# Chunk 0 of a fused attention and gated-MLP kernel: deviations sent through DRAM, k taken row by row, loads and transposes reordered

## The chip, the cores and the metric

The kernel runs on one core of a Trainium2 chip. The metric is the device time of one execution in microseconds. The core's engines are TensorE (PE; its weight loads are shown as PEld), VectorE (DVE), ScalarE (ACT), GpSimd (POOL) and SyncE (SP). Each works through its own instructions in their order and waits on counters (semaphores) that others raise. DMA transfers are issued from the queue of SP, ACT or POOL and raise a counter when they have landed.

## The reference, cut to what matters

```python
# x: 2048 tokens x 1024, 32 heads of 32, window of 8 keys, 2 apart; F = 3584; all bf16
xn  = (x - mean(x)) / sqrt(var(x) + 1e-5)            # layer norm over the 1024
q, k, v = split_heads(xn @ wqkv)                     # wqkv: 1024 x 3072
logits[s, w] = q[s] . k[s - 2 w] / sqrt(32)          # w = 0..7, masked where s - 2 w < 0
s   = (softmax(logits) @ v[s - 2 w]) @ wo
g   = silu((silu(B_x @ w1) * (B_x @ w3)) @ w2)      # here B_x is xn
out = x + s * g
```

## The kernel before

Tokens go in four chunks of 512 (`CH`), a chunk in four tiles of 128 tokens. For each chunk TensorE computes q, k and v, the gate and up products, the down product and the output projection, one behind the other; the windowed attention runs beside it on VectorE, ScalarE and GpSimd from a list of side work with costs and due times (`Side`). The schedule is written out by hand: every engine's order is the order of the source, except that counters, of which the DMA transfers of SP and ACT share eight in turn, are given out when the program is built. A transfer that gets a counter waits until that counter's last transfer has landed.

Chunks 1 to 3 get their normalised, transposed input while the chunk before them runs. Chunk 0 has nothing before it, and its opening (L161 to L204 and L511 to L670) is code of its own. The change lies there alone.

*Loads.* SP issues the transfers in the order of L161 to L166: tiles 0 and 1 of x in two halves each, then the weights of q (wq, four tiles of two rows, a "row" being 128 of the 1024 input features) and of k (wk, likewise), one transfer of 256 KB for a row (`cuts=2`), with tiles 2 and 3 of x in between. Both wq and wk carry the name wq in the profile.

*Tokens 0 to 255 (tiles 0 and 1).* To start before the deviations are known, TensorE transposes the raw tiles, takes off the mean, and the result `xcT` is centred but not divided by the deviation. q and k of these 256 tokens are made from `xcT` by `part` (L602), which for a row `kt` and output groups `js` issues one matmul of 256 columns a group into that group's PSUM bank: eight banks (`banks`), q in the left half of a bank and k in the right. The reciprocal deviations `rs0` (a column of 128 partitions for each tile) must then multiply the columns; `proj_out` (L294) does so on VectorE while it empties the bank, with `R`, a 128 x 256 tile that holds the 256 values in every partition. `R` is made on the chip itself: GpSimd splits each value into three bf16 parts (L618 to L621), VectorE spreads them on diagonals (`dgr`, L627), TensorE sums them over the partitions with three matmuls against ones into a free half of the last bank (L632), and ScalarE copies the bank to `R` (L636).

q runs over all eight rows for all groups (L622 to L626); k over rows 0 to 4 for all groups, and then, group by group, rows 5 to 7, after which the group's bank is emptied (L655 to L661).

*Tokens 256 to 511 (tiles 2 and 3).* These are normalised on VectorE (`stats`, `std` on ScalarE, `recip`, `norm0`) and transposed by DMA into `xnT` (L646), all four tiles from SP in the order 2, 3, 0, 1; behind these stand the loads of v's weights (`wv`, L651) and the next weights. q and k of tokens 256 to 511 then go group by group, 256 columns wide (L662 to L668), into the bank halves that `proj_out` has emptied, and ScalarE empties them again. v follows for all 512 tokens (L673, matmuls at L264), and needs all four tiles of `xnT` and `wv`.

Of the kernel before, what the change touches and what calls it, by code (L numbers as in the profile page):

```python
# [8 lines left out]
FP32 = mybir.dt.float32  # L9
BF16 = mybir.dt.bfloat16  # L10
# [35 lines left out]
def kernel(  # L46
# [11 lines left out]
    nc = tc.nc  # L58
    P = 128
    S, D, F = 2048, 1024, 3584  # L60
    Dh, W, DIL = 32, 8, 2
    KT = D // P
    CH = 512
# [5 lines left out]
    NJ = 8  # L69
# [19 lines left out]
    small = ctx.enter_context(tc.tile_pool(name="small", bufs=4))  # L89
# [5 lines left out]
    blk = ctx.enter_context(tc.tile_pool(name="blk", bufs=9))  # L95
    sm = ctx.enter_context(tc.tile_pool(name="sm", bufs=1))
    ep = ctx.enter_context(tc.tile_pool(name="ep", bufs=2))
    ctx.enter_context(tc.manual_schedule())

    side = Side()  # L100
# [16 lines left out]
    def load_w(n=1, cuts=1, between=None):  # L117
        for _ in range(n):
            item = next(w_next, None)
            if item is None:  # L120
                return
            wt = wstream.tile([P, 2048], BF16, tag="w", name="w" + item[0])
            if item[0] == "q":
                _, t, a = item
                view = wt.rearrange("p (k c) -> p k c", k=2)
                src = wqkv_r[:, 2 * a:2 * a + 2, t * D:(t + 1) * D]
            elif item[0] == "2":
                _, dh, fb = item
                view = wt.rearrange("p (i n) -> p i n", n=512)
                src = w2_r[:, fb * 4:(fb + 1) * 4, dh * 512:(dh + 1) * 512]  # L130
            else:
                view = wt.rearrange("p (k f) -> p k f", k=KT)
                src = (w1_r if item[0] == "1" else w3_r)[:, :, item[1] * 256:(item[1] + 1) * 256]
            step = view.shape[1] // cuts
            for i in range(cuts):
                if i > 0 and between is not None:
                    between()
                nc.sync.dma_start(out=view[:, i * step:(i + 1) * step, :], in_=src[:, i * step:(i + 1) * step, :])  # L138
            w_tiles.append((item, view))
# [14 lines left out]
    x0 = [xp.tile([P, D], BF16, tag="x", name=f"x0_{st}") for st in range(NST)]  # L154

    def load_x0(st, cuts=1):
        w = D // cuts
        for h in range(cuts):
            nc.sync.dma_start(out=x0[st][:, h * w:(h + 1) * w], in_=x_flat[st * P:(st + 1) * P, h * w:(h + 1) * w])  # L159

    load_x0(0, 2)  # L161
    load_x0(1, 2)
    load_w(3, cuts=2)
    load_w(1, cuts=2, between=lambda: load_x0(2))
    load_x0(3)
    load_w(4, cuts=2)  # L166
    eps_t = const.tile([P, 1], FP32, name="eps_t")
    nc.vector.memset(eps_t[:], 1e-5)
    warm = hp.tile([P, CH], BF16, tag="ht", name="warm")
# [3 lines left out]
    ident = const.tile([P, P], BF16, name="ident")  # L173
    nc.gpsimd.memset(ident[:], 0.0)
    nc.gpsimd.affine_select(
        out=ident[:], in_=ident[:], compare_op=ALU.not_equal, fill=1.0,
        base=0, pattern=[[-1, P]], channel_multiplier=1,
    )
    ones_b = hp.tile([P, P], BF16, tag="ht", name="ones_b")
# [4 lines left out]
        out=ident_d[:], in_=ident_d[:], compare_op=ALU.not_equal, fill=-1.0 / D,  # L184
# [5 lines left out]
        out=maskb[:], in_=maskb[:], compare_op=ALU.is_ge, fill=-1.0e9,  # L190
# [17 lines left out]
    def half_stats(x_t, stats, i):  # L208
        nc.vector.bn_stats(out=stats[:, i, :], in_=x_t[:, i * 512:(i + 1) * 512])

    def normalize(x_t, mean, rstd):
        nc.vector.tensor_scalar(
            out=x_t[:], in0=x_t[:], scalar1=mean, scalar2=rstd, op0=ALU.subtract, op1=ALU.mult,
        )
# [74 lines left out]
    def proj_out(t, j, ps, a=0, b=CH, by=None):  # L289
        dst = (qT[:, j, a:b], kT[:, j, HALO + a:HALO + b], vT[:, j, HALO + a:HALO + b])[t]  # L290
        if by is None:
            nc.scalar.copy(out=dst, in_=ps)  # L292
        else:
            nc.vector.tensor_mul(dst, ps, by)  # L294
# [219 lines left out]
    HC = CH // 2  # L514
    xcT = xnT_pool.tile([P, KT, CH], BF16, tag="xnT", name="xcT")
# [6 lines left out]
    V, A = nc.vector.tensor_copy, nc.scalar.copy  # L522
    mv0 = [small.tile([P, 2], FP32, tag="mv0", name=f"mv0_{st}") for st in range(NST)]
    st0 = {st: small.tile([P, 2, nc.vector.BN_STATS_DIM], FP32, tag="st0", name=f"st0_{st}") for st in range(1, NST)}
    rs0 = small.tile([P, NST], FP32, tag="rs0", bufs=1, name="rs0")
    dgs = [hp.tile([P, P], BF16, tag="ht", name=f"dg{st}") for st in range(2)]
    tot = small.tile([P, 1], FP32, tag="tot", bufs=1)
    nm = small.tile([P, 1], FP32, tag="nm", bufs=1)
    rsb = small.tile([P, 3, 2], BF16, tag="rsb", bufs=1, name="rsb")
    rest = small.tile([P, 2], FP32, tag="rest", bufs=1, name="rest")  # L530
    junk = ep.tile([P, D], BF16, tag="gt", bufs=5, name="junk")
    dgr = ep.tile([P, 3, 2, P], BF16, tag="gt", bufs=5, name="dgr")
    R = ep.tile([P, HC], FP32, tag="gt", bufs=5, name="R")

    def stats(st):
        half_stats(x0[st], st0[st], 0)
        half_stats(x0[st], st0[st], 1)
        nc.vector.bn_aggr(out=mv0[st][:], in_=st0[st][:])

    def std(st):  # L540
        nc.scalar.activation(out=rs0[:, st:st + 1], in_=mv0[st][:, 1:2], func=ACTF.Sqrt, bias=eps_t[:], scale=1.0)

    def recip(a, b):
        nc.vector.reciprocal(out=rs0[:, a:b], in_=rs0[:, a:b])

    def norm0(st):
        normalize(x0[st], mv0[st][:, 0:1], rs0[:, st:st + 1])
# [22 lines left out]
    def copy_in(src, st, k0, n, eng):  # L570
# [13 lines left out]
        out=dgs[1][:], in0=ident[:], scalar1=mv0[1][:, 0:1], scalar2=-1.0, op0=ALU.mult, op1=ALU.mult,  # L584
# [14 lines left out]
    banks = [psum_mm.tile([P, CH], FP32, tag="mm", name="ps_qkv") for _ in range(6)]  # L599
    banks[4:4] = [psum_aux.tile([P, CH], FP32, tag="aux", name="ps_qkv") for _ in range(2)]  # L600

    def part(t, kt, js, a, b, first, src):  # L602

        for j in js:
            o = t * HC + a % HC
            nc.tensor.matmul(  # L606
                banks[j][:, o:o + b - a], lhsT=(wq, wk)[t](kt, j), rhs=src[:, kt, a:b],
                start=first, stop=(kt == KT - 1), skip_group_check=True,
            )
# [5 lines left out]
    recip(0, 2)  # L615
    norm0(0)
    norm0(1)
    for i in range(3):  # L618
        nc.gpsimd.tensor_copy(out=rsb[:, i, :], in_=rs0[:, 0:2] if i == 0 else rest[:])
        if i < 2:  # L620
            nc.gpsimd.tensor_sub(rest[:], rs0[:, 0:2] if i == 0 else rest[:], rsb[:, i, :])  # L621
    part(0, 0, range(6), 0, P, True, xcT)  # L622
    part(0, 0, range(6), P, HC, False, xcT)
    part(0, 0, range(6, NJ), 0, HC, True, xcT)
    for kt in range(1, KT):
        part(0, kt, OPEN, 0, HC, False, xcT)  # L626
    nc.vector.tensor_mul(  # L627
        dgr[:].rearrange("p i a b -> p (i a) b"), ident[:].unsqueeze(1).to_broadcast([P, 6, P]),
        rsb[:].rearrange("p i a -> p (i a)").unsqueeze(2).to_broadcast([P, 6, P]),
    )  # L630
    for i in range(3):
        nc.tensor.matmul(  # L632
            banks[NJ - 1][:, HC:CH], lhsT=ones_b[:], rhs=dgr[:, i, :, :].rearrange("p a b -> p (a b)"),
            start=(i == 0), stop=(i == 2), skip_group_check=True,
        )
    A(out=R[:], in_=banks[NJ - 1][:, HC:CH])  # L636
    stats(2)
    std(2)
    stats(3)
    std(3)  # L640
    for st in (2, 3):
        recip(st, st + 1)
        norm0(st)
    xnT = xnT_pool.tile([P, KT, CH], BF16, tag="xnT", name="xnT_0")
    for st in (2, 3, 0, 1):
        nc.sync.dma_start_transpose(out=xnT[:, :, st * P:(st + 1) * P], in_=x0[st][:])  # L646
    wv = []
    for a in range(4):
        if a % 2 == 0:
# [2 lines left out]
        wv.append(two[:, a % 2])  # L652
    wv = by_group(wv)
    load_w(1)
    for kt in range(5):  # L655
        part(1, kt, OPEN, 0, HC, kt == 0, xcT)
    for j in OPEN:
        for kt in range(5, KT):
            part(1, kt, (j,), 0, HC, False, xcT)
        proj_out(0, j, banks[j][:, 0:HC], 0, HC, R[:])  # L660
        proj_out(1, j, banks[j][:, HC:CH], 0, HC, R[:])  # L661
    for t in range(2):  # L662
        for j in OPEN:
            for kt in range(KT):
                part(t, kt, (j,), HC, CH, kt == 0, xnT)
            if j == NJ - 1:
                load_w(4)
            proj_out(t, j, banks[j][:, t * HC:(t + 1) * HC], HC, CH)  # L668
# [3 lines left out]
    for c in range(NCH):  # L672
# [20 lines left out]
        if c + 1 < NCH:  # L693
# [10 lines left out]
            xnT = att["x"]  # L704
# [35 lines left out]
```

## Time and profile before

| What | us |
|---|---|
| median of 3 runs | 814.91 (814.81 to 815.32) |
| the profiled execution | 814.77 |
| its span, first to last instruction | 813.0 |
| start of q and k from `xnT` | 21.55 |
| start of v | 35.52 |
| granted clock of TensorE, share | 0.999 |

The span starts with the first instruction; some 1.8 us of the execution lie around it. Times in the views below are counted from the span's start. "SPq" and "ACTq" are the queues in which SP and ACT issue transfers. In a chain of waits each line is what ended last at that point, in order of time; in the timeline neighbouring instructions of a kind are merged into one line with their number (x3).

### The profile page before, as it was taken

The numbers are of one execution on the slowest core, as the hardware profiler recorded it, in microseconds if no ns is written. First come the engines' busy times: TensorE is split into PE (matmuls) and PEld (weight loads), VectorE is DVE, ScalarE is ACT, GpSimd is POOL, SyncE is SP. The second block draws the span as 40 slices with busy tenths as digits, with TensorE's granted clock in tenths as the row PEclk, the third lists the DMA queues.
The fourth block names the chain that finished last, engine by engine and source line by source line (L and its number), as shares of the span: only waits on it lengthen the run. The fifth ranks groups of instructions, "written<-read, shape, count | busy, mean of one in ns | idle before, by whom it ended". The sixth has DMA issues, their size and how long they took to land.

```text
span 813.0 us, 9680 instructions
## 1 busy us (share of the span) xinstructions
PE 807.7 (99%) x3883; PEld 411.4 (51%) x3883; DVE 473.0 (58%) x488; ACT 187.8 (23%) x310; POOL 93.9 (12%) x180
## 2 busy tenths in 40 slices
PE   9999999999999999999999999999999999999998
PEld 7954444444665444444466444444446644444443
DVE  4489573962239766495124967569411695649632
ACT  3331241012332133101133213310223321311120
POOL 1000404001100122200010022210001003040010
PEclk9999999999999999999999999999999999999999
DMA  9945989842366699984244779996434377687500
GB/s 285 292 122 163 223 203 260 284 145 74 118 189 171 197 208 187 278 266 144 79 151 133 205 195 205 191 319 208 140 91 155 104 207 193 170 227 240 181 31 21
DMA packets 195357, 147.44 MB, mean 181 GB/s; under 512 B 23536, under 2 KB 176240, under 8 KB 195312
## 3 DMA queue, kind: packets, MB, share of 16 engines
q1 hardware_dynamic: 189872, 134.76, 60.3%
q0 software_dynamic: 5440, 12.07, 6.3%
q8 instruction: 30, 0.49, 0.3%
q14 instruction: 15, 0.12, 0.1%
HBM read 130.02 MB, written 4.19 MB: 165 GB/s over the span
## 4 chain that ended last, share of the span: by engine, by line
PE 97%; DMA 1%; SPq 1%; DVE 0%; issue 0%; DVEq 0%
PE gu L264 48%; PE acc L476 21%; PE ps_qkv L264 17%; PE ps_wo L431 7%; PE acc L499 3%; PE ps_qkv L606 2%; DMA wq<-in_A_wqkv_dram 1%; DMA x<-in_A_x_dram 1%; SPq L138 0%; SPq L159 0%; DVE o_t L457 0%; DVE gt L456 0%; DVEq L456 0%
## 5 line engine op out<-in xcount | busy, mean ns | idle before, releaser
L264 PE MATMUL gu<-xnT_next,w 128*128 128x512 bf16 x1344 | 290.6, 379 | 0.0
L264 PEld LDWEIGHTS <-w 128*128 128x128 bf16 x1792 | 175.2, 98 | 211.4
L476 PE MATMUL acc<-w,ht 128*128 128x512 bf16 x784 | 170.4, 379 | 0.0
L270 DVE TENSOR_TENSOR ht<-sg,gu 128x512 bf16<-128x512 bf16 x112 | 75.8, 682 | 110.3 <-PE gu L264 93.7
L268 ACT ACTIVATE sg<-gu 128x512 bf16<-128x512 f32 x112 | 66.1, 597 | 268.9 <-PE gu L264 266.0
L264 PE MATMUL ps_qkv<-xnT_next,wq 128*128 128x512 bf16 x576 | 124.8, 379 | 0.0
L476 PEld LDWEIGHTS <-ht 128*128 128x128 bf16 x784 | 76.7, 98 | 92.5
L321 DVE TENSOR_TENSOR prod<-qT,kT 128x4096 bf16<-128x4096 bf16 x32 | 73.1, 2285 | 80.1 <-ACT kT L292 80.1
L264 PEld LDWEIGHTS <-wq 128*128 128x128 bf16 x576 | 82.6, 143 | 41.8
L264 PE MATMUL gu<-xnT,w 128*128 128x512 bf16 x448 | 96.9, 379 | 0.0
L456 DVE TENSOR_TENSOR gt<-gt,s_sb 128x512 f32<-128x512 f32 x31 | 21.4, 690 | 106.9 <-ACT gt L450 69.2
L352 POOL DMA_DIRECT2D L<-E x64 | 37.2, 587 | 282.8 <-DVE E L336 197.3
L405 DVE TENSOR_TENSOR pv<-Pr,vT 128x4096 bf16<-128x4096 bf16 x28 | 63.0, 2283 | 0.0
L332 DVE TENSOR_TENSOR prod<-prod 128x2048 bf16<-128x2048 bf16 x64 | 61.1, 955 | 1.4
L431 PE MATMUL ps_wo<-wo,oT 128*128 128x512 bf16 (+1 forms) x264 | 56.1, 373 | 0.0
L450 ACT ACTIVATE gt<-acc 128x512 f32<-128x512 f32 x32 | 19.1, 597 | 150.2 <-PE acc L476 128.4
L394 POOL DMA_DIRECT2D Pr<-pb x64 | 36.6, 579 | 107.3 <-DVE pb L386 97.2
L458 POOL DMA_DIRECT2D out_dram<-o_t x28 | 15.3, 546 | 289.3 <-DVE o_t L457 289.3
L431 PEld LDWEIGHTS <-oT 128*128 128x128 bf16 x264 | 25.8, 98 | 29.7
L416 DVE TENSOR_TENSOR oT<-oT,pv 128x4096 bf16<-128x4096 bf16 x16 | 36.6, 2289 | 0.4
L443 ACT CAST s_sb<-ps_wo 128x512 bf16<-128x512 f32 x31 | 18.1, 585 | 66.4 <-PE ps_wo L431 66.4
L606 PEld LDWEIGHTS <-wq 128*128 128x128 bf16 x262 | 28.2, 144 | 0.6 <-DMA wq<-in_A_wqkv_dram 0.5
(82 smaller groups left out, 344.0 us busy)
## 6 DMA issues: line engine op xcount, KB each, us to landing
w<-in_B_w_dram SPq DMA_DIRECT2D x168, 512.0 KB, 5.2
wq<-in_A_wqkv_dram SPq DMA_DIRECT2D x36, 512.0 KB, 3.7
wo<-in_A_wo_dram SPq DMA_DIRECT2D x8, 1024.0 KB, 11.0
wq<-in_A_wqkv_dram SPq DMA_DIRECT2D x16, 256.0 KB, 5.3
L<-E POOLq DMA_DIRECT2D x64, 64.0 KB, 6.7
Pr<-pb POOLq DMA_DIRECT2D x64, 64.0 KB, 6.4
xres<-in_A_x_dram SPq DMA_DIRECT2D x4, 1024.0 KB, 6.8
out_dram<-o_t POOLq DMA_DIRECT2D x28, 128.0 KB, 2.0
```

The costliest lines, as they stand in the source:

```text
L264: nc.tensor.matmul(ps, lhsT=lhs(kt), rhs=rhs(kt), start=(kt == 0), stop=(kt == KT - 1))
L268: nc.scalar.activation(out=sg[:], in_=g_ps[:], func=ACTF.Silu)
L270: nc.vector.tensor_mul(ht[:], sg[:], u_ps[:])
L321: nc.vector.tensor_mul(prod, qT[:], kT[:, :, o:o + CH])
L332: nc.vector.tensor_add(prod[:, 0:n, :], prod[:, 0:n, :], prod[:, n:2 * n, :])
L352: nc.gpsimd.dma_start(out=L4[sq * NH:(sq + 1) * NH, r, :, :], in_=E_r[r, :, :, sq * P:(sq + 1) * P],)
L394: nc.gpsimd.dma_start(out=Pr_r[r, :, :, sq * P:(sq + 1) * P], in_=pb[sq * NH:(sq + 1) * NH, :, :],)
L405: nc.vector.tensor_mul(dst, Pr[:, w, :].unsqueeze(1).to_broadcast([P, NJ, CH]), vT[:, :, o:o + CH])
L416: nc.vector.tensor_add(a, a, b)
L431: nc.tensor.matmul(ps[:, 0:w], lhsT=oT[:, j, st * P:(st + 1) * P], rhs=was[dh][:, j, n0:n0 + w], start=(j == 0), stop=(j == NJ - 1),)
L476: nc.tensor.matmul(accs[st][:], lhsT=hts[f][:, st * P:(st + 1) * P], rhs=w2t[:, i, :], start=(f == 0), stop=(f == FT - 1),)
L606: nc.tensor.matmul(banks[j][:, o:o + b - a], lhsT=(wq, wk)[t](kt, j), rhs=src[:, kt, a:b], start=first, stop=(kt == KT - 1), skip_group_ch ...
```

## The change

- The loads of wq are not broken any more by tiles 2 and 3 of x: all four wq tiles come first, tile 2 stands between the two rows of the first wk tile, tile 3 after it, and then the other wk rows.
- `R` is made by DMA: ScalarE's queue stores the 2 x 128 reciprocal deviations to a tile in DRAM (`rrow`, element by element transposed), and loads it back with every partition reading the same 256 values. The GpSimd split, `dgr`, the three matmuls and ScalarE's copy are gone.
- VectorE takes tile 3's statistics in two halves, with tile 2's reciprocal and normalisation between them.
- The transpose of tile 3 is issued from ScalarE's queue; tiles 2, 0 and 1 stay on SP.
- k of tokens 0 to 255 goes over rows 0 to 6 for all groups, then row 7 group by group.
- q of tokens 256 to 511 in groups 0 and 1 is made in two steps of 128 columns, tile 2 first for both groups, then tile 3.

```diff
+    dram = ctx.enter_context(tc.tile_pool(name="dram", bufs=1, space=bass.MemoryType.DRAM))
...
-    load_w(3, cuts=2)
+    load_w(4, cuts=2)
     load_w(1, cuts=2, between=lambda: load_x0(2))
     load_x0(3)
-    load_w(4, cuts=2)
+    load_w(3, cuts=2)
...
-    for i in range(3):
-        nc.gpsimd.tensor_copy(out=rsb[:, i, :], in_=rs0[:, 0:2] if i == 0 else rest[:])
-        if i < 2:
-            nc.gpsimd.tensor_sub(rest[:], rs0[:, 0:2] if i == 0 else rest[:], rsb[:, i, :])
+
+    rrow = dram.tile([2, P], FP32, name="rrow")
+    nc.scalar.dma_start(out=rrow.rearrange("s p -> p s"), in_=rs0[:, 0:2])
+    nc.scalar.dma_start(out=R[:], in_=rrow.rearrange("s p -> (s p)").unsqueeze(0).to_broadcast([P, HC]))
...
-    nc.vector.tensor_mul(
-        dgr[:].rearrange("p i a b -> p (i a) b"), ident[:].unsqueeze(1).to_broadcast([P, 6, P]),
-        rsb[:].rearrange("p i a -> p (i a)").unsqueeze(2).to_broadcast([P, 6, P]),
-    )
-    for i in range(3):
-        nc.tensor.matmul(
-            banks[NJ - 1][:, HC:CH], lhsT=ones_b[:], rhs=dgr[:, i, :, :].rearrange("p a b -> p (a b)"),
-            start=(i == 0), stop=(i == 2), skip_group_check=True,
-        )
-    A(out=R[:], in_=banks[NJ - 1][:, HC:CH])
     stats(2)
     std(2)
-    stats(3)
+    half_stats(x0[3], st0[3], 0)
+    recip(2, 3)
+    norm0(2)
+    half_stats(x0[3], st0[3], 1)
+    nc.vector.bn_aggr(out=mv0[3][:], in_=st0[3][:])
     std(3)
-    for st in (2, 3):
-        recip(st, st + 1)
-        norm0(st)
+    recip(3, 4)
+    norm0(3)
...
     for st in (2, 3, 0, 1):
-        nc.sync.dma_start_transpose(out=xnT[:, :, st * P:(st + 1) * P], in_=x0[st][:])
+        q = nc.scalar if st == 3 else nc.sync
+        q.dma_start_transpose(out=xnT[:, :, st * P:(st + 1) * P], in_=x0[st][:])
...
-    for kt in range(5):
+    for kt in range(KT - 1):
         part(1, kt, OPEN, 0, HC, kt == 0, xcT)
     for j in OPEN:
-        for kt in range(5, KT):
-            part(1, kt, (j,), 0, HC, False, xcT)
+        part(1, KT - 1, (j,), 0, HC, False, xcT)
         proj_out(0, j, banks[j][:, 0:HC], 0, HC, R[:])
         proj_out(1, j, banks[j][:, HC:CH], 0, HC, R[:])
+
+    for st in (2, 3):
+        for j in range(2):
+            for kt in range(KT):
+                part(0, kt, (j,), st * P, (st + 1) * P, kt == 0 and st == 2, xnT)
     for t in range(2):
         for j in OPEN:
             for kt in range(KT):
-                part(t, kt, (j,), HC, CH, kt == 0, xnT)
+                if t == 1 or j >= 2:
+                    part(t, kt, (j,), HC, CH, kt == 0, xnT)
```

In the changed program as it is built, the waits of the moved transfers are these. The store of `rrow` waits for the last wq row (they share a counter) and for the reciprocal; the load of `R` for tile 3 of x (likewise) and for the store. The transposes stand in SP's queue in the order 2, 0, 1. The one of tile 3, in ScalarE's queue behind the roots of tiles 2 and 3, waits for the transposes of tiles 2 and 0 to have landed; the one of tile 1 waits for tile 3's.

More of the change, by code (lines that the diff above doesn't have):

```diff
@@ L528 @@
     nm = small.tile([P, 1], FP32, tag="nm", bufs=1)
-    rsb = small.tile([P, 3, 2], BF16, tag="rsb", bufs=1, name="rsb")
-    rest = small.tile([P, 2], FP32, tag="rest", bufs=1, name="rest")
     junk = ep.tile([P, D], BF16, tag="gt", bufs=5, name="junk")
-    dgr = ep.tile([P, 3, 2, P], BF16, tag="gt", bufs=5, name="dgr")
     R = ep.tile([P, HC], FP32, tag="gt", bufs=5, name="R")
```

## The prediction, made before the changed kernel was run

> **What bounds the kernel now.** I read the page first, for the engine that is full, then the chain that ended last, then the timeline of the first 48 us, where the change lies, and last the single transfers of that stretch.
>
> ```profile
> PE 807.7 (99%) x3883; PEld 411.4 (51%) x3883; DVE 473.0 (58%) x488; ACT 187.8 (23%) x310; POOL 93.9 (12%) x180
> ```
>
> TensorE is busy all but about 5 us of the 813.0 us span. A change to the opening can gain only what TensorE loses or wastes there, and can lose whatever it newly waits there. The chain of waits of the first 60 us, in order of time (start, length, what):
>
> ```profile
> 6.88 5.88 DMA x<-in_A_x_dram
> 12.77 0.02 issue
> 12.79 6.25 DMA wq<-in_A_wqkv_dram
> 19.04 0.05 issue
> 19.09 16.60 PE ps_qkv L606 x150
> 35.68 13.81 PE ps_qkv L264 x64
> ```
>
> The last row of wk lands at 19.04 and TensorE goes on at 19.09; from there it never stops. The timeline (start, length, engine, line, operation, idle before):
>
> ```profile
> 13.69 0.49 PE L632 MATMUL ps_qkv<-dgr,ones_b 128*128 128x256 bf16 x3
> 14.02 4.75 PE L606 MATMUL ps_qkv<-xcT,wq 128*128 128x256 bf16 x42
> ...
> 14.49 0.66 ACT L541 ACTIVATE rs<-mv,eps_t 128x1 f32<-128x1 f32 x2
> ...
> 15.48 0.15 DVE L544 RECIPROCAL rs<-rs 128x1 f32<-128x1 f32 x1
> 15.60 5.96 SPq L646 DMA_TRANSPOSE xnT<-x  x4
> ...
> 19.09 2.62 PE L606 MATMUL ps_qkv<-xcT,wq 128*128 128x256 bf16 x22 [0.32 <-DMA wq<-in_A_wqkv_dram]
> ...
> 21.55 14.14 PE L606 MATMUL ps_qkv<-xnT,wq 128*128 128x256 bf16 x128
> ```
>
> Two losses are seen: the three matmuls that broadcast R (13.69 to 14.02, 0.33 us) and the stop before 19.09. The 42nd matmul began at 18.50 and 128 of them run from 21.55 to 35.52, so one takes 0.109 us; the stop is 18.61 to 19.09, 0.48 us, and the restart costs 0.06. So 0.87 us is all there is to gain. What must be ready in time is the transposed xnT of tokens 256 to 511, wanted at 21.55. Its transfers (duration of the issue; time to landing):
>
> ```profile
> L646 SPq DMA_TRANSPOSE xnT<-x x4: 1300/1346/1760, 15.6 to 20.2; - x4
> DMA to landing us min/median/max: 3.1/3.6/4.3
> ```
>
> Asked one by one, tile 2 is issued at 15.60 and lands after 4.3 (19.9), tile 3 at 17.06 after 3.8 (20.8), and the fourth at 20.22 after 3.1 (23.4). Four in one queue overlap: a tile costs about 1.2 us more, not 3.
>
> **The change part by part.**
>
> *Removed.* The R matmuls: 0.33 us of TensorE. The five GpSimd instructions of the split and VectorE's `dgr` product (0.96 us at 11.04) lie under the q matmuls, which run to 13.69; ScalarE's copy of R (0.38) goes too. With k run over seven rows for all groups, the eighth row is reached 56 x 0.109 = 6.1 us after 13.69, at 19.8. It lands at about 19.0, so the stop goes: 0.54. TensorE would reach xnT at 21.55 - 0.87 = 20.68.
>
> *Added on TensorE.* Groups 0 and 1 of q are cut in two columns halves: 32 matmuls 128 wide for 16 of 256. The 128-wide ones at 7.0 us start 0.063 apart: 32 x 0.063 - 16 x 0.109 = +0.26 us. Gain net of it: 0.61.
>
> *Moved: loads.* Places in SP's queue are 0.66 us apart (four issues from 9.47 to 12.12). The last wq row goes one place forward, from 6.40 + 5.7 = 12.1 to 11.4. Tiles 2 and 3 go two places back: from 11.4 to 12.8 and from 12.8 to 14.1. The last wk row keeps its place. VectorE has `dgr` less and is free, so statistics of tile 2 end at 12.8 + 1.3 + 0.2 = 14.35.
>
> *Added on ScalarE's queue.* The store of rs0 waits for the last wq row (it has that transfer's completion counter), 11.45. The read of R waits for tile 3 (14.1) and for the store. Behind it in ScalarE's strict order stands the root of tile 2, hence reciprocal, normalisation and the first transpose. The nearest row of a store to DRAM is the output's, 1.6/2.0/4.3 us to landing, with 1 KB runs and little else on the engines; no row has 256 pieces of 4 bytes beside a full load stream. The bounds are 11.45 + 1.6 = 13.1 and, by the far row of the shuffle beside a load stream (64 KB each, median 6.7), 18.2. I take 3.1 us, 14.6, between the output's median and its worst, since the bytes are few but the rings are full. Then the read is issued by 15.05 (0.43, as SP's), root 0.32, and from reciprocal to transpose 0.78 as before (14.82 to 15.60): the transpose of tile 2 starts at 16.2 against 15.60. If the store costs nothing, VectorE's first half of tile 3 sets it: 15.8. At 18.2 it is 19.8. R itself lands some 3 to 4.5 us after its issue, 18 to 19.5, when VectorE first wants it at 19.9 (19.45 before).
>
> *Moved: the transposes.* This decides. Tile 3 goes to ScalarE's queue, and the built program orders it there behind the completion of both transposes that SP issues first, tiles 2 and 0; tile 1, on SP, then waits for tile 3. What was a 1.2 us step of a pipeline becomes a full transfer after two others have landed. From first issue to the second landing took 5.24 us beside the last wk rows (15.60 to 20.84), and 4.50 without loads (third and fourth, 18.87 to 23.37); I take 4.9. A lone one took 3.1 to 3.15, with a neighbour still ahead of it; bounds 2.8 (its 1.33 us issue and some 1.5 of landing after it, as for the 128 KB loads, 2.07 less 0.40) and 6.2 (the median of the later chunks, with weights ahead in the same ring, which ScalarE's ring has not); I take 3.1 and 0.05 for the wake. Tile 3 lands at 16.2 + 4.9 + 3.15 = 24.25.
>
> TensorE finishes wk at 20.68, has 16 half matmuls on tile 2 (1.0 us, with tile 2 there at about 20.3 and bank 0 emptied by 20.4), and stands from 21.7 to 24.3. Then 0.11 for wake and restart, 16 x 0.063 + 112 x 0.109 = 13.23: v starts at 37.6 instead of 35.52, **+2.07 us**. The removed 0.87 is inside that sum; while tile 3 is the last to come, it buys nothing.
>
> *Queued behind.* SP holds tile 1 and the four wv loads until 24.3: wv is issued from 25.7 to 27.7 and, at the worst landing before (8.2), there at 35.9, wanted from 37.6. The next w tiles wait for slots that TensorE frees, as before. From v on TensorE is the bound, so the shift is carried to the end. Profiled 814.77 (span 813.0 and 1.8 around it) + 2.07 = 816.84; the median of the runs, 814.91, is 0.14 higher: **817.0 us**.
>
> The rule of the Trainium skill that bears on it ("DMA: Bandwidth & Descriptors", Rules for kernel authors) speaks against the change: transposes from two queues have to be serialized, the later waiting for the earlier one's completion. The trace of before, with one queue, cannot show it. By the rule the sum is the one above; without it, it would be the first rival's.
>
> **The rivals.**
>
> *A, not slower: tile 3 lands before it is missed.* It must land by 21.7. If the second queue overlapped the first, with its own issue at about 17.6 (normalisation of tile 3) and 3.8 as before, it would land at 21.4. Then v starts at 20.68 + 2.01 + 12.23 = 34.92, -0.60: 814.3. For it: before, tile 3 landed 0.9 after tile 2. Against: the two waits in the program. The point from which it decides is 21.7. 8%.
>
> *B: the round trip through DRAM is what ends last.* With the store at 16.5 or later the root of tile 2 waits, everything after it slides one for one, and TensorE's gap passes 4 us: +3.7 and more, 818.6. For: 256 pieces of 4 bytes, and ScalarE blocked in order. Against: the small output stores. 12%.
>
> *C: TensorE's clock drops in the gap.* At the start of the trace, after idling, matmuls of 512 columns start 0.42 apart ((2.91 - 1.22) / 4), and in v 13.81 / 64 = 0.216; the half pace lasted some 4 us. A gap that restores it costs up to 2 us more: 819.0. Against: the gap is 2.6 us. 6%.
> The Trainium skill ("TensorE: Matmul & The Clock Gate", The HAM clock gate) puts the drop after an idle window of about 3.4 us; by that the gap forecast is too short, and one from 21.7 past 25.1 would do it.
>
> **How the numbers follow.** Forecast (the serialized transposes, v late by 0.9 to 3.2 us) 74%, A 8%, B 12%, C 6%. Range: from +0.9 (tile 2 at 15.8, 4.5 and 2.8) to +4.0, inside B and C: 815.8 to 818.9; it leaves out A, a little under the forecast, and the far ends of B and C, two in ten. A measurement of this kernel tells 0.2%, 1.63 us, from no change. Slower by that needs tile 3 after 23.8: three quarters of the forecast, B and C, 0.73. A and the rest of the forecast lie within 0.2%: 0.25. A gain of 1.63 is out of reach, since 0.87 is all that TensorE loses: 0.02.
>
> **What would show it.** TensorE's longest wait is for an xnT transpose, after 16 half matmuls, ending at 24.3, and not for wk; the stop at 18.6 is gone; ScalarE's transpose is issued after 20.8. ScalarE's root of tile 2 stands behind the read of R. v begins near 37.6. I am wrong if tile 3 lands before 21.7, if TensorE stands longer on bank 0 (R late) than on xnT, or if the gap after v moves by another amount than the start of v.

## The result, and the profile after

| | us |
|---|---|
| before, median of 4 runs beside those of after | 814.86 (814.56 to 815.32) |
| after, median of 4 runs | 825.43 (823.59 to 825.97) |
| ratio, 95% interval | 1.0125 (1.0113 to 1.0138) |
| profiled execution of after, its span | 825.07, 823.3 |
| start of q and k from `xnT`: before, after | 21.55, 26.89 |
| start of v: before, after | 35.52, 45.96 |

The change costs 10.6 us where 2.1 were forecast. All of it lies in the opening: from the start of v to the last matmul 773.46 us pass in both traces, and v starts 10.44 us later. TensorE's work has hardly changed, its span has grown:

```profile
PE 807.5 (98%) x3824; PEld 413.3 (50%) x3896; DVE 472.5 (57%) x487; ACT 187.8 (23%) x309; POOL 92.9 (11%) x175
```

The chain of waits of after, 5 to 50 us (start, length, what):

```profile
5.94 6.11 DMA wq<-in_A_wqkv_dram
...
12.12 9.02 DMA rrow<-rs
...
21.16 4.65 DMA R<-rrow
...
27.90 3.18 DMA xnT<-x
31.09 0.04 issue
31.13 14.99 PE ps_qkv L604 x128
```

Before, the chain went from the last wk row straight to TensorE at 19.09. Now it goes through the store of 256 numbers (1 KB), which takes 9.02 us, and then through ScalarE's transpose of tile 3. The piece `R<-rrow` is put on the chain because VectorE empties the banks with R; the transpose of tile 2 lands at 26.84 by another way, as the timeline shows (in brackets: idle before, and what ended it):

```profile
12.12 0.40 ACTq L618 DMA_DIRECT2D rrow<-rs  x1
...
19.15 1.09 PE L604 MATMUL ps_qkv<-xcT,wq 128*128 128x256 bf16 x8 [1.73 <-DMA wq<-in_A_wqkv_dram]
...
21.16 4.51 PE L604 MATMUL ps_qkv<-xcT,wq 128*128 128x256 bf16 x24 [0.91 <-DMA wq<-in_A_wqkv_dram]
...
21.55 0.29 ACT L539 ACTIVATE rs<-mv,eps_t 128x1 f32<-128x1 f32 x1 [12.52 <-DMA rrow<-rs]
...
22.65 9.69 SPq L638 DMA_TRANSPOSE xnT<-x  x3
...
26.89 1.21 PE L604 MATMUL ps_qkv<-xnT,wq 128*128 128x128 bf16 x16 [1.23 <-DMA xnT<-x]
27.90 1.35 ACTq L638 DMA_TRANSPOSE xnT<-x  x1
...
31.13 14.99 PE L604 MATMUL ps_qkv<-xnT,wq 128*128 128x128 bf16 x128 [3.03 <-DMA xnT<-x]
```

Read from top to bottom: the root of tile 2 stands in ScalarE's order behind the load of R, which waits for the store, so ScalarE is idle for 12.5 us and the first transpose is issued at 22.65 (before: 15.60). TensorE has meanwhile stopped twice for wk, whose last four rows land at 19.11, 21.11, 21.49 and 22.15 (before: 17.04, 17.68, 18.34 and 19.04). Then it stops for tile 2, and after 16 half matmuls 3 us more for tile 3. The 128 matmuls after that take 14.99 us, the same 128 in run e2 below 13.38: for 3.41 us of them the granted clock is half (31.79 to 35.20 in the views of the last section).

Four causes can be told apart here: the store is slow; while it is under way the weights are late; the two transpose queues are strung together; the clock drops. The experiments take them one by one.

### The profile page after: what moved, and what is told of

The parts are those of the page before. It is cut to its first block, busy times and chain, and to the rows that moved or that the text cites. A ratio compares the mean times of both kernels' runs of the same rounds, so it can differ in the third digit from the quotient of the medians.

```text
span 823.3 us, 9636 instructions
## 1 busy us (share of the span) xinstructions
PE 807.5 (98%) x3824; PEld 413.3 (50%) x3896; DVE 472.5 (57%) x487; ACT 187.8 (23%) x309; POOL 92.9 (11%) x175
## 4 chain that ended last, share of the span: by engine, by line
PE 91%; DMA 5%; DVE 2%; issue 1%; SPq 1%; ACT 0%; DVEq 0%; ACTq 0%
PE gu L265 43%; PE acc L477 20%; PE ps_qkv L265 17%; PE ps_wo L432 7%; PE acc L500 3%; PE ps_qkv L604 2%; DMA wq<-in_A_wqkv_dram 1%; DMA rrow<-rs 1%; DMA xnT_next<-x_t 1%; DMA x_t<-in_A_x_dram 1%; DMA R<-rrow 1%; SPq L139 0%; DMA xnT<-x 0%; DVE mx L380 0%; DVE mx L384 0%
## 5 line engine op out<-in xcount | busy, mean ns | idle before, releaser
L265 PEld LDWEIGHTS <-wq 128*128 128x128 bf16 x576 | 82.6, 143 | 41.8
L604 PEld LDWEIGHTS <-wq 128*128 128x128 bf16 x278 | 30.4, 147 | 9.4 <-issue 3.1
L444 ACT CAST s_sb<-ps_wo 128x512 bf16<-128x512 f32 x31 | 18.2, 586 | 66.4 <-PE ps_wo L432 65.3
## 6 DMA issues: line engine op xcount, KB each, us to landing
wo<-in_A_wo_dram SPq DMA_DIRECT2D x8, 1024.0 KB, 11.6
```

Of the source, the lines that this page charges most:

```text
L265: nc.tensor.matmul(ps, lhsT=lhs(kt), rhs=rhs(kt), start=(kt == 0), stop=(kt == KT - 1))
L604: nc.tensor.matmul(banks[j][:, o:o + b - a], lhsT=(wq, wk)[t](kt, j), rhs=src[:, kt, a:b], start=first, stop=(kt == KT - 1), skip_group_ch ...
```

## The experiments

### The store or the two queues

Three kernels are after with a part undone, a fourth is before with one part done.

`e1_R_onchip`: R is made on the chip as before, everything else stays as in after.

```diff
-    nc.scalar.dma_start(out=rrow.rearrange("s p -> p s"), in_=rs0[:, 0:2])
-    nc.scalar.dma_start(out=R[:], in_=rrow.rearrange("s p -> (s p)").unsqueeze(0).to_broadcast([P, HC]))
+    for i in range(3):
+        nc.gpsimd.tensor_copy(out=rsb[:, i, :], in_=rs0[:, 0:2] if i == 0 else rest[:])
...
+    A(out=R[:], in_=banks[NJ - 1][:, HC:CH])
```

> The changed kernel with R made on the chip as before (GpSimd split, dgr, three matmuls, copy); loads, statistics, k row by row and the two transpose queues as changed. If the store to DRAM is the cause and the two queues cost what was forecast: tile 2's transpose starts at 15.8 to 16.2, tile 3 lands near 24, v starts near 37.3, 816.4 to 816.9 us. If the store explains everything and two queues cost nothing: v starts at 35.0 to 35.3, 814.3 to 814.7 us. If the store is a bystander: 823 to 826 us as the changed kernel.

`e2_tr_sp`: all four transposes on SP again, R through DRAM.

```diff
-        q = nc.scalar if st == 3 else nc.sync
-        q.dma_start_transpose(out=xnT[:, :, st * P:(st + 1) * P], in_=x0[st][:])
+        nc.sync.dma_start_transpose(out=xnT[:, :, st * P:(st + 1) * P], in_=x0[st][:])
```

> The changed kernel with all four transposes on SP, R still through DRAM. If the store sets the start of the first transpose (22.65 in the changed kernel) and the pipeline of one queue returns: tile 3 lands near 27.8, v starts near 41.2, 820 to 821 us, or up to 1.5 us more if the clock still drops. If the two queues are the larger part: 815 to 817 us.

`e3_onchip_tr_sp`: both of these edits.

> The changed kernel with R on the chip and all transposes on SP: what is left is the load order, the interleaved statistics, k row by row to the seventh row and the 128-column steps. If store and queues are the only losses, the stop before 19.09 is gone, the R matmuls (0.33 us) are back, 32 half matmuls cost 0.26: v starts near 35.2, 814.5 us (-0.3). If the later loads of tiles 2 and 3 make the transposes late: v at 36 or later, 815.5 us or more.

`e4_dram_only`: before, with nothing but the store and the load of R in place of the split, `dgr`, the three matmuls and the copy.

> The kernel before with one part of the change alone: R through DRAM. If the store beside the load stream costs some 9 us and blocks ScalarE's roots of tiles 2 and 3: the first transpose starts at 20 or later instead of 15.6, v starts at 39 or later, 818 us or more, and the wk rows land up to 4 us late. If the store is only slow where it waits for a load's counter or for tile 3: within 1 us of before, 814 to 816 us.

| | R through DRAM | transposes on | median, us | ratio to before (95%) | start of v |
|---|---|---|---|---|---|
| after | yes | SP and ACT | 825.43 | 1.0125 (1.0113 to 1.0138) | 45.96 |
| e1 | no | SP and ACT | 816.55 | 1.0021 (1.0011 to 1.0032) | 39.41 |
| e2 | yes | SP | 820.81 | 1.0072 (1.0052 to 1.0092) | 41.24 |
| e3 | no | SP | 814.83 | 0.9996 (0.9986 to 1.0006) | 36.30 |
| e4, before's order | yes | SP | 820.38 | 1.0067 (1.0047 to 1.0087) | 41.22 |

The median of before was 815.06 beside the four experiments; e2 and e4 ran twice each, e1 eight and e3 ten times. The profiled execution of e1 was its slowest (818.65, with a stop for wq of 0.95 us that no other trace has), so its start of v is about 2 us above what its median stands for. In e3's, TensorE began with q at 7.21 us instead of 6.50, after a late rise of its clock (last section); that is 0.7 of the 0.8 us by which its v is later than before's.

The store alone costs 5.75 us (e2) and 5.3 (e4), in the new order and in the old one alike. The two queues alone cost 1.5 (e1). With neither, nothing is left that a measurement can tell from before (e3). Both together cost 10.6, some 3.3 more than the sum of the two. Where these come from shows in the timeline of e2, with one queue:

```profile
26.48 1.21 PE L604 MATMUL ps_qkv<-xnT,wq 128*128 128x128 bf16 x16 [2.03 <-DMA xnT<-x]
28.03 13.38 PE L604 MATMUL ps_qkv<-xnT,wq 128*128 128x128 bf16 x128 [0.34 <-DMA xnT<-x]
```

Tile 3 follows tile 2 by 1.55 us, in after by 4.24 (26.89 to 31.13). In e1 too tile 3 is strung behind, but there TensorE still has wk's rows to do while part of this passes; in after they have run out. That is 2.7 us between after and e2. The last stretch, from tile 3 to v, takes 13.21 us in e2 and 14.83 in after, 1.6 more. The remaining 0.4 lies at tile 2: its transpose starts at about the same time (22.65, in e2 22.76) but takes 4.2 us instead of 3.7; why is open. The sum is 4.7, the difference of the two starts of v.

### The half clock

`e10_fill_gap`: after, with 26 matmuls that nobody reads between the steps of tile 2 and of tile 3, where TensorE stood still.

```diff
     for st in (2, 3):
+        if st == 3:
+            for _ in range(26):
+                nc.tensor.matmul(
+                    banks[2][:, 0:HC], lhsT=warm[:, 0:P], rhs=warm[:, 0:HC],
+                    start=True, stop=True, skip_group_check=True,
+                )
         for j in range(2):
```

> The changed kernel with 26 matmuls of 256 columns added that nobody reads, after tile 2's half matmuls, where TensorE waits for tile 3 from 28.1 to 31.1. If the clock drop after that gap costs 1.5 us: the granted clock stays at 1.0 after tile 3 lands, v starts 13.3 us after the landing instead of 14.9, 823.6 to 824.2 us. If the slow stretch has another cause (banks, ScalarE): 825 us or more, and the stretch stays.

Median 823.71, ratio 1.0101 (1.0087 to 1.0115): 1.7 us less than after, with 2.8 us of work more. The second half-clock stretch is gone, and from the start on tile 3 (30.48) to v (43.69) it takes 13.2 us as in e2. So the drop cost 1.6 to 1.7 us. The first stretch (21.25 for 3.41 us in this trace, 21.55 in after) remains. In after it cost nothing: the work under it ended at 25.66, and tile 2 landed at 26.84 anyway.

### What the store itself costs, and what it does to others

`e5_side_packed`: before, with the change's store added and its result read by nobody. No instruction waits for it.

```diff
+    side_d = dram.tile([2, P], FP32, name="side_d")
+    nc.scalar.dma_start(out=side_d.rearrange("s p -> p s"), in_=rs0[:, 0:2])
```

> The kernel before with the change's store added (256 pieces of 4 bytes, packed into 1 KB of DRAM) and read by nobody; R is made on the chip. If the store holds up the loads by itself: it lands after about 9 us and the last wk rows land at 20 to 22 us instead of 19.0. If the loads are late only through the order of the change: wk as before, 19 to 19.5 us.

`e6_side_spread`: the same 256 numbers, each 512 bytes from the next.

```diff
+    side_d = dram.tile([2, P, 128], FP32, name="side_d")
+    nc.scalar.dma_start(out=side_d[:, :, 0:1].rearrange("s p o -> p s o"), in_=rs0[:, 0:2].unsqueeze(2))
```

> As the run with the packed side store, with the 256 pieces of 4 bytes 512 bytes apart in DRAM. If writes into the same 1 KB get in each other's way: lands in 2 to 5 us, wk near 19.0 to 19.5. If each piece costs the same anywhere beside the load stream: 9 us and wk at 20 to 22 as the packed one.

`e7_side_eight`: the same 1 KB as 128 pieces of 8 bytes, the two numbers of a partition side by side.

```diff
+    side_d = dram.tile([P, 2], FP32, name="side_d")
+    nc.scalar.dma_start(out=side_d[:], in_=rs0[:, 0:2])
```

> As the run with the packed side store, with 128 pieces of 8 bytes in the same 1 KB. If the number of pieces sets it: the excess over some 3 us is halved, lands after 5 to 6.5 us. If the 1 KB they share sets it whatever their number, or the wait in the rings: 8 to 9 us.

The transfers of 9 to 24 us in the traces of e5, e6 and e7, in this order (last column: median us from issue to landing; wq stands for wk too):

```profile
wq<-in_A_wqkv_dram SPq DMA_DIRECT2D x6, 256.0 KB, 8.3
side_d<-rs ACTq DMA_DIRECT2D x1, 1.0 KB, 9.6
```

```profile
wq<-in_A_wqkv_dram SPq DMA_DIRECT2D x6, 256.0 KB, 5.8
side_d<-rs ACTq DMA_DIRECT2D x1, 1.0 KB, 5.2
```

```profile
wq<-in_A_wqkv_dram SPq DMA_DIRECT2D x7, 256.0 KB, 5.3
side_d<-rs ACTq DMA_DIRECT2D x1, 1.0 KB, 5.8
```

With the packed store the six loads take 8.3 us instead of 5.3 to 5.8, though they come from another queue and nothing waits for the store. The last wk row lands at 22.22 instead of 19.04: 2.5 us of that are its longer flight (8.8 for 6.3), 0.6 its later issue. v starts at 38.70 instead of 35.52, and the one execution took 818.76 against 815.03 for before on the same chip; 0.9 us of it are a stop near 352 us, far from the edit, which stays unexplained. With the spread one v starts at 35.52, as before (815.88, with a like stop of 1.1 us near 349), and with the 8-byte pieces at 35.67 (814.83). Each of the three ran once, but the flight of the last wk row says the same in every run: 7.7 to 9.1 us beside a packed store (after, e2, e4, e5, e10), 5.2 to 6.8 without a store or beside another form (before, e1, e3, e6 to e9, e11). So neither a store at this place, nor one of 256 pieces, nor one of 4-byte pieces holds up the weights: 4-byte pieces side by side do.

`m1_quiet`: before, with a chain of stores and loads in ScalarE's queue behind the last output, when nothing else runs. Each load waits for the store ahead of it, and each store for the load.

```diff
+    packed = dram.tile([2, P], FP32, name="packed")
+    nc.scalar.dma_start(out=packed.rearrange("s p -> p s"), in_=t[:, 0:2])
+    t = back(packed.rearrange("s p -> (s p)").unsqueeze(0), HC)
...
+    spread = dram.tile([2, P, 128], FP32, name="spread")
+    nc.scalar.dma_start(out=spread[:, :, 0:1].rearrange("s p o -> p s o"), in_=t[:, 0:2].unsqueeze(2))
+    t = back(spread[0:1, 0, 0:1], 1)
```

> The kernel before, with stores to DRAM and broadcast loads in ScalarE's queue after its last output, one at a time, each waiting for the one before: 2 rows of 512 bytes; 256 pieces of 4 bytes packed into 1 KB (the change's store); 128 pieces of 8 bytes in 1 KB; 256 pieces of 4 bytes 512 bytes apart; 128 pieces of 4 bytes packed. It computes the reference and some more transfers. If the load stream is what made the store slow: every one lands in about 2 us. If many small writes into the same 1 KB are slow by themselves: the packed one takes 5 us or more, 128 of 8 bytes about half of the excess, the spread one about 2 us. If each small piece costs the same wherever it goes: packed and spread both 5 us or more.

Its timeline from 809 to 850 us:

```profile
811.59 0.38 ACTq L721 DMA_DIRECT2D packed<-back  x1
819.60 0.34 ACTq L714 DMA_DIRECT2D back<-packed  x1
...
830.95 0.38 ACTq L727 DMA_DIRECT2D spread<-back  x1
832.53 0.33 ACTq L714 DMA_DIRECT2D back<-spread  x1
```

From a store's issue to that of the load behind it: 8.0 us for 256 packed numbers, 6.9 for 128 packed ones (835.04 to 841.95), 2.85 for 128 pieces of 8 bytes (824.20 to 827.05), 1.6 for 256 numbers spread out. So 8 of the 9.0 us in after are the store's own and would be there on an idle chip; the loads around it add one. The bytes don't decide, and the number of pieces doesn't alone: half the pieces take 1.1 us less, and the same 256 pieces apart from each other a fifth. Nor is it the sending: by the trace's packet records all 256 packets are through 1.15 us after the issue in both forms. What differs is the time until the sixteen completion signals that raise the store's counter have come: 817.07 to 819.53 us for the packed store and 832.34 to 832.51 for the spread one.

### Whether a better store saves the change

`e8_eight_tr_sp`: e2 with the store of e7; VectorE reads R in the other order (`by.rearrange("p (q s) -> p s q", s=2)`).

```diff
-    rrow = dram.tile([2, P], FP32, name="rrow")
-    nc.scalar.dma_start(out=rrow.rearrange("s p -> p s"), in_=rs0[:, 0:2])
+    rrow = dram.tile([P, 2], FP32, name="rrow")
+    nc.scalar.dma_start(out=rrow[:], in_=rs0[:, 0:2])
```

> The changed kernel with all transposes on SP and rrow laid out so that the store is 128 pieces of 8 bytes (R then holds the two tiles' values in turn, and VectorE reads it in steps of two). If the pieces of 4 bytes in one 1 KB are the cost: the store takes 5.8 us beside the loads as in the side store, the read of R goes out at 17.3, the first transpose at 18.9, tile 3 lands near 24, v starts near 37.3, 816.5 to 817.5 us against 820.8 with 4 bytes; the wk rows land by 19.5. If any trip through DRAM costs the same here: 820 to 821.5.

Median 816.67 against 814.89 for before, ratio 1.0021 (1.0011 to 1.0032); e2 had 820.81. The stop for wk is gone. From its chain of waits:

```profile
11.85 5.73 DMA rrow<-rs
...
19.08 4.11 DMA xnT<-x
```

The store takes 2.85 us on an idle chip and 5.73 here, beside the loads, and the transposes still start 3.5 us later than before.

`e9_eight_roots_first`: e8, with the load of R behind the roots of tiles 2 and 3, so that these don't wait for the store.

```diff
-    nc.scalar.dma_start(out=R[:], in_=rrow.rearrange("p s -> (p s)").unsqueeze(0).to_broadcast([P, HC]))
...
     std(3)
+    nc.scalar.dma_start(out=R[:], in_=rrow.rearrange("p s -> (p s)").unsqueeze(0).to_broadcast([P, HC]))
```

> As the run with pieces of 8 bytes, and the load of R moved behind the roots of tiles 2 and 3 in ScalarE's queue. If ScalarE's blocked queue is what makes the transposes late: the first starts near 16 again, and R becomes the last to come (store 17.3, load 4.7, 22), bank 0 is emptied at 22.4, v near 36.5, 815.5 to 816.3 us. If not the queue but the traffic delays them: the first transpose stays near 18.9, 816.5 us or more.

Median 817.59 (816.32 to 819.61 in 8 runs), ratio 1.0035 (1.0023 to 1.0046), above the 815.5 to 816.3 expected. The profiled execution is the fastest of the eight, and no trace shows what the others lose besides. In it the transposes start at 15.75, as before, but R is now late itself: its load is issued at 17.57 and lands at 21.93, and TensorE waits for a bank that VectorE empties with it. The timeline:

```profile
22.83 14.55 PE L605 MATMUL ps_qkv<-xnT,wq 128*128 128x128 bf16 x144 [1.77 <-DVE kT L296]
```

The wait has only changed its name. Two trips through DRAM, 5.8 and 4.4 us, don't fit between the issue of the store (11.68) and the first use of R (19.45 before). The reciprocals are ready at 9.5; until 11.6 the store waits for the last wq row, whose counter it shares. A store with a counter of its own was not run. An estimate from these times has R landing near 19.8, and in e11's order below VectorE first uses it at 20.25; so whether a trip through DRAM can be hidden here stays open.

### Whether the rest is worth anything

`e11_no_halves`: e3 without the 128-column steps; what is left of the change is the order of the loads, the interleaved statistics and k up to the seventh row.

```diff
-    for st in (2, 3):
-        for j in range(2):
-            for kt in range(KT):
-                part(0, kt, (j,), st * P, (st + 1) * P, kt == 0 and st == 2, xnT)
...
-                if t == 1 or j >= 2:
-                    part(t, kt, (j,), HC, CH, kt == 0, xnT)
+                part(t, kt, (j,), HC, CH, kt == 0, xnT)
```

> What is left of the change without the DRAM trip, the second transpose queue and the 128-column steps: load order, interleaved statistics, k row by row to the seventh row; R on the chip. If TensorE's stop before the last wk row was worth its 0.54 us and the transposes still come in time: 814.4 to 814.7 us beside 814.9 to 815.1 of before (ratio 0.9993 to 0.9997). If tile 3's transpose, later by the later loads, is now missed: 815.0 us or more.

In the profiled execution, the fastest of the eleven, TensorE stands still for some 0.1 us in all between 15 and 40 us, v starts at 35.04 (before: 35.52) and the span is 812.5 (813.0). Of these 0.48 us 0.16 come from an earlier start of q (6.34 for 6.50); the other 0.32 are the stop before wk's last row, and no more. The median of 11 runs is 815.16 (814.27 to 816.65) against 814.89, ratio 1.0001 (0.9992 to 1.0010): no gain that can be told from nothing. No version here is shown to beat before.

## Why the prediction was right in direction and wrong in size

- **The step that failed is a term of the sum: the store's duration.** "I take 3.1 us, 14.6, between the output's median and its worst, since the bytes are few but the rings are full." It took 9.02, to 21.14, past the upper bound of 18.2 too. The rows it was bounded by have longer pieces (1 KB in the output's, 256 bytes in the shuffle's, which doesn't go to DRAM); the prediction said itself that no row has pieces of 4 bytes, and then went by bytes and load. m1 shows 8 of the 9 us on an idle chip, where e7's form takes 2.85 and e6's 1.6. The first transpose came at 22.65 instead of 16.2: 5.9 from the store and 0.67 from its later issue (12.12 for 11.45), less 0.14 on the way.
- **The chain behind the store was right link by link.** From first transpose to the second landing 5.10 us (4.9 forecast), the lone transpose of tile 3 3.2 (3.15). So tile 3 landed at 31.09 instead of 24.25, 6.84 later, of which 6.45 come from the late first transpose. Rival B, the round trip that ends last, names the mechanism that took place; its 818.6 was worked out for a store at 16.5, which wasn't late enough either (the forecast's own chain gives 818.9 for that store).
- **"The last wk row keeps its place" was wrong**: 22.15 instead of 19.0, so the stop that was to go became two, 1.73 and 0.91 us. Of the 3.1 us 1.8 are a longer flight (8.1 for 6.3) and 1.3 a later issue (14.1 for 12.8). No step priced what a store does to the loads beside it; e5 shows 2.5 us of longer flight for that alone. In after it ran beside the wait for the transposes and so added nothing.
- **Rival C came true on top of B.** The clock dropped after the gap and cost 1.6 to 1.7 us (e10), inside the "up to 2 us". The gap was 3.03 us, barely above the 2.6 that was held too short. The sum: 6.84 for tile 3 and 1.53 for the stretch behind it (14.87 from landing to v, 13.34 forecast) make the 8.37 us by which v missed 37.59.
- **Right, and shown:** the two queues cost 1.5 us by themselves (e1), and TensorE's longest wait is for `xnT` after 16 half matmuls. The gain from k's seven rows is small (e11: 0.32 us of the earlier start of v in one execution) and not seen in the medians. Everything from v on moved by one amount, 10.44.
- **Open:** why 4-byte writes side by side in DRAM are slow. The Trainium skill ("DMA: Bandwidth & Descriptors", Specifications and Rules for kernel authors) has read-modify-write for transfers below 512 bytes and one descriptor for each element where the last dimension isn't contiguous. The trace agrees that small pieces can be dear, but both statements hold for the spread store as well, which took 1.6 us against 8.0 in m1, so they are not enough. That pieces which share a line of memory wait for one another would fit all four stores of m1; it is argued, not shown.

## What to carry to other kernels

Price a small transfer by the shape of its pieces in memory, not by its bytes: if no row of the trace has that shape, measure it alone and beside the load stream before anything is put behind it. An in-order queue that holds a wait for a transfer also holds what stands behind it (here a root, and so every transpose); look whether that can go ahead, and then whether the transfer's own user becomes the next one late, as in e9. Costs on two links don't add where TensorE's remaining work covers one of them: undo each alone and both together before dividing up a loss.

## What the runs showed of the hardware that was not expected

**A 1 KB store can hold up loads of 256 KB in another queue.** In after 175 to 197 of the 2 KB packets of the weights started in each microsecond from 9 to 16 us, and 21 to 29 from 17 to 21; one took 3.66 us, where 0.084 is usual. In before the rate falls at 17 us too, but there only 31 packets are left, in after 115. The DMA engines were not full then: over 18.14 to 21.55 they moved 50 GB/s at a busy share of 0.29 (first line below).

**The clock goes by windows with a fixed grid, and a window need not be idle.** In after and in e10, every change of the granted clock lies a multiple of 3.413 us after the first rise to full speed in that trace (4.49 in after; 21.55, 24.96, 31.79 and 35.20 are 5, 6, 8 and 9 steps further). Cut by that grid (stretch, length, TensorE's busy time with its instructions, granted clock, DMA share, GB/s), after shows

```profile
18.14:21.55 3.41, 1.49 (x12) 1.00 0.29 50
...
24.96:28.38 3.42, 1.91 (x22) 1.00 0.82 155
28.38:31.79 3.41, 0.66 (x11) 1.00 0.41 77
31.79:35.20 3.41, 3.41 (x22) 0.50 0.70 135
```

e10 in the stretch that its added matmuls filled

```profile
28.08:31.49 3.41, 3.35 (x39) 1.00 0.41 77
```

and e2 in its emptiest one

```profile
18.92:22.33 3.41, 1.60 (x15) 1.00 0.19 38
```

A window in which TensorE was busy for 1.49 us (44%) or 0.66 (19%) was followed by one at half clock, as was one of 1.39 (41%) in e10; windows of 1.60 (47%, e2), 1.82 (53%, e4) and 1.91 (56%, after) were not. The ends of the kernels narrow it down: e11's window with 1.54 us (45%) was followed by full clock, before's with 1.37 (40%) by half. So the limit lay between 44 and 45% in these traces, by the busy time that the profile models. e2's single stop of 3.34 us was split between two windows and cost no clock; the two stops for wk in after are shorter (1.73 and 0.91 us), but 1.92 us of idle time fell into one window. Where the grid lies differs from run to run (the first rise came between 4.19 and 7.19 us), and it moves the opening: two matmuls of 512 columns near 5.2 us take 0.59 us in e11, after its rise at 5.10, and 1.01 in e3, which rises at 7.06. So by this reading the same gap can cost 1.7 us in one run and nothing in the next; no pair of traces here shows that. The Trainium skill ("TensorE: Matmul & The Clock Gate", The HAM clock gate) has the free-running window of 3413 ns, and the trace agrees to the hundredth; that the window before a drop is idle, as its table puts it, the traces do not bear out.
